# Attention units in nine steps, each at a place between two blocks of the mixture's matmuls

## Chip, cores and metric

One core of one Trainium2 chip runs the whole program. The metric is the device time in microseconds (us), the median of several executions; the profile is of one execution.

## What is computed

Three stages in a row: windowed attention with four sink tokens, a maximum-of-three mixture with an output matrix, and a routed set of eight experts. The change touches the first two.

```python
def _attn_ref(q, k, v, n_sink, window):          # 4 batches, 8 heads, 768 tokens, 64 wide; 4 sinks, window 128
    scores = scale * np.matmul(q, k.transpose(0, 1, 3, 2))
    keep = is_sink | in_window
    scores = np.where(keep, scores, -1000000000.0)
    a = np.exp(scores - np.max(scores, axis=-1, keepdims=True))
    a = a / (np.sum(a, axis=-1, keepdims=True) + 1e-09)
    return np.matmul(a, v)
def _moe_ref(x, w1, w2, w3, w_out):              # x: 3072 tokens x 512
    h = np.maximum(np.maximum(x @ w1, x @ w2), x @ w3)   # 768 wide
    return h @ w_out
def _moe2_ref(x, w_gate, w1, w2):                # 8 experts of 384 tokens each, by descending logit
    ...
        h = np.maximum(x[mask] @ w1[e], 0.0)
        out[mask] = h @ w2[e]
```

## The kernel before

The 3072 tokens are handled as eight groups (0 to 7) of 384 tokens: half a batch each. A group needs four **units** of attention, one for each pair of heads, which give its four tiles `x0` to `x3`, and then its **mixture**. Products are made of fp32r parts: each operand is split into a high part (a rounded copy) and a low part (the rest), and three matmuls stand for one product.

A unit (`att`, L608 to L612) runs through `load` (DMAs of k, q, v and of the sinks' v, `vns`, from the SP queue), `prep` (the splits `kh`, `kz`, `qs` of k and q, `vsp` of v, and on POOL `vk` of the sinks' v, L99 to L102), `score` (six score blocks into PSUM tiles `ps`, copied into `T` by ACT and DVE), `soft` (the row maximum on DVE, six exponentials on ACT, the reciprocal on DVE, the scaling of `T` on POOL) and `pv`. In `pv` TensorE turns `T` into `pt` and `pp`; DVE multiplies `pp` by masks into `A` (L163), ACT copies it into `H`, POOL subtracts into `L`, and TensorE multiplies `H`, `L` and the sinks' part `psb` into `po`, which ACT and DVE write to `x`. `pt`, `pp` and `po` have one PSUM tile each, `ps` three; the tile `A` has one buffer from group 2's units on; `kn`, `qn`, `vn`, `vns` have one buffer each, `H`, `L`, `vsp` and `qs` two.

The mixture of a group is `group` (L249): 18 blocks of 12 matmuls of 384 columns into the two PSUM tiles `mm`, three blocks for each of six slices `f`, the first taken out by ACT (L270) and the others by DVE (L271), after which ACT and DVE split the maximum into `hh` and `hl` (L275, L276). Then comes `x2` (L280): three row tiles times two halves, six blocks of 18 matmuls of 260 columns (L290), each taken out by ACT into `xo` and then by DVE into `LG`; `xo` has one buffer and is stored to `x2d` from SP's queue. Group 0's own `x2` runs after group 1's, from a copy of its maxima that is read back (`reload`, L300: the tile `hm` with two buffers, split by L306 and L307). Groups 6 and 7 make logits first and their `x2` later.

The order within each engine's queue is set by a scheduler that goes through the emitted program by readiness and priority. Before the change the units of group g+1 are emitted whole inside the mixture of group g, ahead of its slices 0, 1, 3 and 4, and with a raised priority of 60 instructions, so that the scheduler may draw their parts forward:

```python
late=list(range(cnt.get(f'a{g+1}',-1)+1,4)) if g+1<NG else []
def between(f):
    if f in spread and late: late.pop(0); emit(f'a{g+1}',True)
```

Of the kernel before, what the change touches and what calls it, by code (L numbers as in the profile page):

```python
# [22 lines left out]
def f32(ap): return ap.bitcast(FT)  # L23
# [3 lines left out]
class Attn:  # L27
# [55 lines left out]
    def prep(s,u):  # L83
# [26 lines left out]
    def score(s,u):  # L110
        nc=s.nc; w=s.w; hf=u['hf']
# [3 lines left out]
        for i in range(3):  # L115
            first = hf==0 and i==0
# [31 lines left out]
    def pv(s,u,x):  # L148
        nc=s.nc; w=s.w; T=u['T'].rearrange('p u j -> p (u j)'); hf=u['hf']; nb=u['nb']; nat=u['nat']
        psk=s.pst.tile([128,512],FT,name="pt")  # L150
        for i in range(3): flip(nc,psk[:,i*128:(i+1)*128],T[:,264*i+128:264*i+256],s.ident)
        PB=s.pb[u['n']%2]
        nc.scalar.activation(PB[0:8],psk[0:8,:384],AF.Copy)
        nc.vector.tensor_tensor(PB[32:40],psk[0:8,:384],f32(PB[0:8]),op=OP.subtract)
# [3 lines left out]
        for h in range(2):  # L158
            pt=s.psp.tile([128,512],FT,name="pp")
            for i in range(3):  # L160
                flip(nc,pt[:,i*128:(i+1)*128],T[:,i*264+136*h:i*264+136*h+128],s.ident)
            A=s.two(dict(n=u['n']*2+h),[128,3,2,128],FT,"A")
            nc.vector.tensor_tensor(A,pt[:,:384].rearrange("p (i q) -> p i q",q=128)[:,:,None,:].to_broadcast([128,3,2,128]),  # L163
                s.ul[:,None,:,:].to_broadcast([128,3,2,128]),op=OP.mult)
            Af=A.rearrange("p i u q -> p (i u q)")
            a=slice(64*h,64*h+64); o=slice(64-64*h,128-64*h)
            if nat:
                if h==0:
                    po=s.psv.tile([128,512],FT,name="po")
                    for a_ in range(2): nc.tensor.matmul(po[:,:384],u['VK'][:,a_,:],PB,start=(a_==0),stop=False,skip_group_check=True)  # L170
                for c,n,q,blk in jobs:
                    nc.tensor.matmul(po[a,q:q+n],u['vn'][:,blk,h,:],Af[:,c:c+n],start=False,stop=True,skip_group_check=True)
                if h==1: nc.scalar.activation(x,po[:,:384],AF.Copy)
                continue
            H=w.tile([128,768],FR,name="H"); L=w.tile([128,768],FR,name="L")
            nc.scalar.activation(H,Af,AF.Copy)  # L176
            nc.gpsimd.tensor_tensor(L,Af,f32(H),op=OP.subtract)  # L177
            po=s.psv.tile([128,512],FT,name="po")
            for part in (H,L):
                for j,(c,n,q,blk) in enumerate(jobs):  # L180
                    nc.tensor.matmul(po[:,q:q+n],u['VS'][:,blk,128*h:128*h+128],part[:,c:c+n],start=(part is H and j==0),stop=False,skip_group_check=True)  # L181
            nc.tensor.matmul(po[:,:384],u['VK'][:,h,:],PB,start=False,stop=True,skip_group_check=True)
            nc.scalar.activation(x[a,:],po[o,:384],AF.Copy)
            nc.vector.tensor_tensor(x[a,:],po[a,:384],x[a,:],op=OP.add)
# [561 lines left out]
```

## Time and profile before

| | |
|---|---|
| median of 3 runs | 1030.28 us (1025.59 to 1030.44) |
| the profiled execution: its own time | 1030.27 us |
| the profiled execution: span of the core | 1028.5 us, mean granted TensorE clock 0.974 |
| busy share of the span: PE, DVE, ACT, POOL | 92%, 69%, 52%, 34% |
| start of group 1's `x2` (first L290 matmul), us from the span's start | 188.44 |
| start of the read-back `x2` of group 0 | 212.34 |
| start of the mixtures of groups 2 to 6 | 244.36, 321.20, 398.03, 468.70, 538.10 |
| start of the `x2` of groups 2 to 5 | 299.05, 373.55, 448.49, 517.69 |
| start of the mixture of group 7 | 582.48 |

The starts are those of the first matmul of each part in the timeline of TensorE. The share of busy time alone doesn't say much here, since the attention and mixture stretches and the later experts have different limits; the table of stretches further down cuts the profile at these starts.

### The profile page before, as it was taken

What the parts mean: (1) busy time and instruction counts of PE and PEld (TensorE: products, weight loads), DVE (VectorE), ACT (ScalarE), POOL (GpSimd) and SP (SyncE); (2) the same over time, 40 slices, a digit from 0 to 9 for tenths busy, and PEclk for the clock granted to TensorE, in tenths of its full rate; (3) what the DMA queues carried; (4) which work ended last, traced back from release to release, by engine and by line L of the source; (5) the groups of instructions that cost most, each with busy time, mean ns of one, the idle gap of its engine ahead of it and who ended that gap; (6) DMA issues with size and microseconds to landing.
All of it is one profiled execution on the core that took longest, in us unless ns stands there. A gap on an engine that the chain in (4) does not pass through costs nothing.

```text
span 1028.5 us, 18554 instructions
## 1 busy us (share of the span) xinstructions
PE 947.7 (92%) x6633; PEld 864.2 (84%) x6633; DVE 711.3 (69%) x1775; ACT 535.8 (52%) x1418; POOL 344.7 (34%) x307
## 2 busy tenths in 40 slices
PE   4879899979999989999999999798989899999996
PEld 3568799879999989989999998786768778788896
DVE  8989876888887884776534344787768788783330
ACT  5667655888788785786452211343333343344431
POOL 4677473145645533435332000101111121133431
PEclk9999999989999999999999999999999999999999
DMA  6543501222112111111010000425243453444420
GB/s 209 156 137 124 164 28 62 74 95 75 46 44 78 48 48 42 54 56 43 13 43 1 1 2 22 149 83 164 84 125 111 134 164 114 132 146 153 154 103 31
DMA packets 47085, 90.32 MB, mean 88 GB/s; under 512 B 6320, under 2 KB 17328, under 8 KB 46992
## 3 DMA queue, kind: packets, MB, share of 16 engines
q1 hardware_dynamic: 42288, 75.11, 23.8%
q0 software_dynamic: 3840, 12.45, 3.5%
q10 hardware_dynamic: 864, 1.57, 0.4%
q8 instruction: 52, 0.85, 0.3%
q14 instruction: 41, 0.34, 0.1%
HBM read 75.48 MB, written 13.76 MB: 87 GB/s over the span
## 4 chain that ended last, share of the span: by engine, by line
PE 61%; DVE 15%; issue 8%; DMA 7%; ACT 6%; POOL 2%; SPq 0%; another core or an unknown queue 0%; POOLq 0%; DVEq 0%; ACTq 0%
PE mm L268 23%; PE mm L576 8%; PE acc L569 8%; PE mm L290 7%; PE po L181 3%; DMA sa<-in_u_dram 2%; PE rc L377 2%; DMA xg<-x2d,idx 2%; PE pt L25 2%; DVE cA L223 1%; DMA st<-in_words_dram 1%; PE pp L25 1%; ACT T_w L144 1%; DVE qs L97 1%; DVE m L141 1%
## 5 line engine op out<-in xcount | busy, mean ns | idle before, releaser
L177 POOL TENSOR_TENSOR L<-A_w,H 128x768 fp32r<-128x768 f32 x46 | 87.5, 1902 | 127.0 <-ACT H L176 98.5
L271 DVE TENSOR_TENSOR hm<-mm,hm 128x384 f32<-128x384 f32 x96 | 53.1, 554 | 61.2 <-PE mm L268 60.1
L290 PE MATMUL mm<-woh,hh 128*128 128x260 f32 (+1 forms) x288 | 85.3, 298 | 5.2 <-DVE LG L293 4.2
L290 PE MATMUL mm<-woh,hl 128*128 128x260 f32 (+1 forms) x288 | 83.7, 295 | 3.9 <-DVE hl L307 2.5
L290 PE MATMUL mm<-wol,hh 128*128 128x260 f32 (+1 forms) x288 | 83.0, 290 | 0.0
L569 PE MATMUL acc<-wbh,hl 128*128 128x512 f32 x192 | 78.0, 406 | 0.5 <-DVE hl L580 0.5
L569 PE MATMUL acc<-wbl,hh 128*128 128x512 f32 x192 | 77.9, 406 | 0.0
L534 POOL DMA_INDIRECT xg<-x2d,idx x24 | 27.4, 1140 | 150.7 <-DVE idx L502 46.6
L569 PE MATMUL acc<-wbh,hh 128*128 128x512 f32 x192 | 77.4, 403 | 0.0
L522 ACT ACTIVATE wah<-sa 128x512 fp32r<-128x512 f32 x64 | 40.4, 631 | 70.1 <-PE mm L576 36.7
L588 POOL DMA_INDIRECT out_dram<-og,idx x24 | 24.5, 1020 | 141.0 <-ACT og L587 138.0
L522 ACT ACTIVATE wbh<-sb 128x512 fp32r<-128x512 f32 x64 | 40.4, 631 | 59.4 <-PE acc L569 54.1
L268 PE MATMUL mm<-xh,w1h 128*128 128x384 f32 x192 | 66.5, 346 | 1.5 <-DVE hm L271 0.7
L580 DVE SCALAR_TENSOR_TENSOR hl<-mm,hh 128x384 fp32r<-128x384 f32 x64 | 35.5, 555 | 46.8 <-ACT hh L579 45.2
L268 PE MATMUL mm<-xh,w2h 128*128 128x384 f32 x192 | 66.5, 347 | 1.4 <-ACT hm L270 1.4
L268 PE MATMUL mm<-xh,w0h 128*128 128x384 f32 x192 | 66.3, 345 | 0.0
L268 PE MATMUL mm<-xl,w0h 128*128 128x384 f32 x192 | 64.9, 338 | 1.2 <-DVE xl L257 1.2
L268 PE MATMUL mm<-xh,w1l 128*128 128x384 f32 x192 | 65.2, 340 | 0.0
L268 PE MATMUL mm<-xl,w1h 128*128 128x384 f32 x192 | 65.2, 339 | 0.0
L268 PE MATMUL mm<-xl,w2h 128*128 128x384 f32 x192 | 64.7, 337 | 0.0
L268 PE MATMUL mm<-xh,w0l 128*128 128x384 f32 x192 | 64.7, 337 | 0.0
L268 PE MATMUL mm<-xh,w2l 128*128 128x384 f32 x192 | 64.6, 337 | 0.0
(308 smaller groups left out, 3103.2 us busy)
## 6 DMA issues: line engine op xcount, KB each, us to landing
sa<-in_u_dram SPq DMA_DIRECT2D x64, 256.0 KB
sb<-in_u_dram SPq DMA_DIRECT2D x64, 256.0 KB
st<-in_words_dram SPq DMA_DIRECT2D x24, 512.0 KB
qn<-in_q_dram SPq DMA_DIRECT2D x24, 192.0 KB
x2d<-xo SPq DMA_DIRECT2D x18, 256.0 KB
kn<-in_k_dram SPq DMA_DIRECT2D x12, 264.0 KB
vn<-in_v_dram SPq DMA_DIRECT2D x12, 256.0 KB
kn<-in_k_dram SPq DMA_DIRECT2D x12, 198.0 KB
```

Source lines behind the costliest of these rows:

```text
L25: nc.tensor.transpose(out,x,f32(ident))
L177: nc.gpsimd.tensor_tensor(L,Af,f32(H),op=OP.subtract)
L181: nc.tensor.matmul(po[:,q:q+n],u['VS'][:,blk,128*h:128*h+128],part[:,c:c+n],start=(part is H and j==0),stop=False,skip_group_check=True)
L268: nc.tensor.matmul(ps[:,:384],s.W[i][a][:,p,f*128:(f+1)*128],X[p][b],start=(n==0),stop=(n==11)); n+=1
L271: else: nc.vector.tensor_tensor(m,ps[:,:384],m,op=OP.max)
L290: nc.tensor.matmul(ps[:,:n],H[f][a][:,t*128:(t+1)*128],s.WO[b][:,f,u,:n],start=(k==0),stop=(k==17)); k+=1
L522: nc.scalar.activation(h,src,AF.Copy)
L534: nc.gpsimd.indirect_dma_start(out=g,out_offset=None,in_=s.x2d[0:first or 3072],in_offset=bass.IndirectOffsetOnAxis(ap=idx[:,t:t+1],axis=0 ...
L569: nc.tensor.matmul(acc[t],H[f][a][:,t*128:(t+1)*128],W[f][1][b],start=(f==0 and n==0),stop=(f==F-1 and n==2)); n+=1
L576: nc.tensor.matmul(ps[:,:384],W[f][0][a][:,k,:],X[k][b],start=(n==0),stop=(n==11)); n+=1
L580: nc.vector.scalar_tensor_tensor(l,ps[:,:384],0.0,f32(h),op0=OP.max,op1=OP.subtract)
L588: st=nc.gpsimd.indirect_dma_start(out=s.out,out_offset=bass.IndirectOffsetOnAxis(ap=idx[:,t:t+1],axis=0),in_=o,in_offset=None)
```

## The change

`pv` is cut into `turned` (the transposes, `A`, `H`, `L`, and now also the making of `vk`) and `pv` proper (the matmuls into `po` and their eviction), each once for each of the pair's two heads, and `score` yields between its three parts. A unit becomes a generator of nine steps: load, prep, three of score (the third with soft), two of turned, two of pv. The steps stand at places 0, 2, 4, 5, 6, 10, 11, 14 and 15 counted from the unit's start; units of groups 3 to 7 start six places apart. A place is the point ahead of one block of the mixture: 18 in `group` and six in `x2`, 24 in a group. What a step emits on TensorE gets an order edge behind the last matmul emitted before it; the raised priority is gone for these units. The read-back `x2` of group 0 has no places. Groups 0 to 2 are emitted as before, apart from the new order of the statements inside a unit.

```diff
     def score(s,u):
...
         for i in range(3):
+            if i: yield
...
+    def turned(s,u,h):
+        nc=s.nc; w=s.w; T=u['T'].rearrange('p u j -> p (u j)'); nat=u['nat']
+        if h==0:
+            VK=u['VK']=s.vk[u['n']%2]
...
+            nc.gpsimd.tensor_copy(hi,u['sv'])
+            nc.gpsimd.tensor_tensor(lo,u['sv'],f32(hi),op=OP.subtract)
+            psk=s.pst.tile([128,512],FT,name="pt")
...
+    def unit(s,b,hf,p,native,main,xs):
+
+        u=s.load(b,hf,p,native); yield
+        s.prep(u); yield
+        yield from s.score(u)
+        s.soft(u); yield
+        s.turned(u,0); yield
+        s.turned(u,1); yield
+        x=main.tile([128,384],FT,name=f"x{p}")
+        s.pv(u,x,0); yield
+        s.pv(u,x,1); xs.append(x)
...
         for f in range(6):
-            if between is not None: between(f)
             m=main.tile([128,384],FT,name="hm",bufs=2)
             for i in range(3):
                 ps=s.mm.tile([128,512],FT,name="mm")
                 n=0
+                if between is not None: between()
...
-    def x2(s,H,t0,LG,x2d,n=260,pool=None,keep=None):
+    def x2(s,H,t0,LG,x2d,n=260,pool=None,keep=None,between=None):
...
+                if between is not None: between()
...
+        todo=[]; clock=[0]
+        STEPS=(0,2,4,5,6,10,11,14,15)
+        def plan(g,start):
+            for p in range(4):
+                U=unit(g,p); todo.extend((start+6*p+t,g,p,U) for t in STEPS)
+            todo.sort(key=lambda x: x[0])
+        def slot(g=None):
+
+            while todo and (todo[0][0]<=clock[0] or any(x[1]==g for x in todo)):
+                with tc.issue_after(M.mm_.ins): next(todo.pop(0)[3],None)
+            if g is None: clock[0]+=1
...
+                    clock[0]=24
+                    for G in range(3,NG): plan(G,24*G-36-6*(G==NG-1))
```

Every engine has as many instructions as before, and up to the start of group 1's `x2` all five queues stand in the same order.

First place, DVE during the read-back of group 0 (`hl3` and `hl4` are low parts of the read-back maxima; `kz`, `qs`, the predicated copies and `m` belong to the splits, scores and row maximum of a unit). Before:

```order
L307 TENSOR_TENSOR hl3_2313<-hm_2310,hh3_2312 128x384
L135 COPY_PREDICATED T_w_2672<-ca_95,ps_2688 128x128
L95 TENSOR_TENSOR kz0b_1618<-kn_3030,kh0_x_3038 64x528
L135 COPY_PREDICATED T_w_2672<-ca_95,ps_2693 128x128
L97 TENSOR_TENSOR qs0_3040<-qn_3032,qs0_3040 64x384
L95 TENSOR_TENSOR kz1b_1619<-kn_3030,kh1_x_3039 64x528
L163 TENSOR_TENSOR A_w_1846<-pp_1842,ul_98 128x768
L135 COPY_PREDICATED T_w_2672<-ca_95,ps_2698 128x128
L97 TENSOR_TENSOR qs1_3041<-qn_3032,qs1_3041 64x384
L154 TENSOR_TENSOR psb0_105<-pt_2548,psb0_105 8x384
L141 TENSOR_REDUCE m_2703<-T_w_2672 128x6
L307 TENSOR_TENSOR hl4_2319<-hm_2316,hh4_2318 128x384
```

And with the change, same engine and place:

```order
L327 TENSOR_TENSOR hl3_2456<-hm_2453,hh3_2455 128x384
L158 TENSOR_TENSOR psb0_105<-pt_2346,psb0_105 8x384
L164 TENSOR_TENSOR A_w_1835<-pp_1831,ul_98 128x768
L327 TENSOR_TENSOR hl4_2462<-hm_2459,hh4_2461 128x384
L327 TENSOR_TENSOR hl5_2468<-hm_2465,hh5_2467 128x384
```

Eight DVE instructions of group 3's units have left the stretch between `hl3` and `hl4`; TensorE has 24 score matmuls fewer between the read-back `x2`'s start and the mixture of group 2.

Second place, TensorE in the `x2` of group 3, from the end of its first two blocks (`hl5` closes both) to the third block (`mm_4201`, which takes the PSUM tile of the first). Before:

```order
L290 MATMUL mm_4178<-woh_1466,hl5_4153 128x260
L181 MATMUL po_4414<-H_4410,vsp_4328 128x128
L181 MATMUL po_4414<-H_4410,vsp_4328 128x256 x2
L181 MATMUL po_4414<-H_4410,vsp_4328 128x128
L181 MATMUL po_4414<-L_4411,vsp_4328 128x128
L181 MATMUL po_4414<-L_4411,vsp_4328 128x256 x2
L181 MATMUL po_4414<-L_4411,vsp_4328 128x128
L182 MATMUL po_4414<-psb0_105,vk0_103 128x384
L126 MATMUL ps_5423<-kh1_x_5398,qs1_5400 128x132
L127 MATMUL ps_5423<-kz1b_1619,qs1_5400 128x132
L126 MATMUL ps_5428<-kh0_x_5397,qs0_5399 128x260
L127 MATMUL ps_5428<-kz0b_1618,qs0_5399 128x260
```

And with the change:

```order
L310 MATMUL mm_4234<-woh_1466,hl5_4178 128x260
L189 MATMUL po_4259<-H_4115,vsp_3841 128x256 x2
L189 MATMUL po_4259<-H_4115,vsp_3841 128x128
L310 MATMUL mm_4257<-woh_1466,hh0_3643 128x260
L310 MATMUL mm_4257<-wol_1467,hh0_3643 128x260
L310 MATMUL mm_4257<-woh_1466,hl0_3644 128x260
```

The score matmuls ahead of the third block are gone, and the matmuls into `po` are cut in two, the second part inside the fourth block.

Third place, TensorE in the mixture of group 4 with the change, between two blocks and inside the next (`ps` are scores of one unit, `po` belongs to an older one):

```order
L287 MATMUL mm_4582<-xh3_4474,w1l_121 128x384
L124 MATMUL ps_4636<-kh0_w_4521,qs0_4523 128x260
L125 MATMUL ps_4636<-kz0_111,qs0_4523 128x260
L287 MATMUL mm_4625<-xh0_4462,w2h_122 128x384
L287 MATMUL mm_4625<-xl0_4463,w2h_122 128x384
L287 MATMUL mm_4625<-xh0_4462,w2l_123 128x384
L124 MATMUL ps_4641<-kh1_w_4522,qs1_4524 128x260
L125 MATMUL ps_4641<-kz1_112,qs1_4524 128x260
```

Pieces of a unit that stood next to each other before, several score blocks at once, now come one or two at a time between or inside blocks.

## Rows read from the trace of the kernel before

**Rows 1.** Stretches from group 1's `x2` to group 7's mixture, cut at the starts above

```profile
core 0: us, PE busy (x) PEld busy (x) DVE busy (x) ACT busy (x) POOL busy (x), PEclk, DMA share, GB/s
188.44:212.34 23.90, 21.20 (x158) 20.20 (x157) 19.53 (x38) 20.45 (x66) 9.69 (x7) 0.93 0.24 70
212.34:244.36 32.02, 26.23 (x179) 24.14 (x178) 26.53 (x48) 25.82 (x76) 13.24 (x11) 0.89 0.30 93
244.36:299.05 54.69, 54.69 (x364) 54.37 (x363) 46.34 (x93) 42.79 (x118) 30.67 (x28) 1.00 0.16 47
299.05:321.20 22.15, 20.84 (x169) 20.17 (x168) 18.00 (x40) 20.81 (x67) 10.03 (x8) 1.00 0.27 85
321.20:373.55 52.35, 51.88 (x328) 50.72 (x327) 43.47 (x76) 38.36 (x114) 24.37 (x20) 1.00 0.17 47
373.55:398.03 24.48, 21.96 (x157) 20.99 (x156) 14.05 (x36) 17.44 (x54) 9.56 (x9) 0.86 0.20 60
398.03:448.49 50.46, 50.46 (x328) 50.29 (x326) 36.23 (x72) 35.12 (x101) 19.78 (x19) 1.00 0.16 46
448.49:468.70 20.21, 18.51 (x147) 17.52 (x146) 13.65 (x32) 15.95 (x46) 8.83 (x7) 1.00 0.20 61
468.70:517.69 48.99, 48.99 (x314) 48.71 (x313) 30.26 (x55) 30.86 (x94) 20.07 (x17) 1.00 0.08 24
517.69:538.10 20.41, 18.73 (x142) 18.41 (x142) 7.68 (x17) 8.02 (x18) 8.59 (x8) 0.92 0.13 41
538.10:582.48 44.38, 44.38 (x271) 43.52 (x270) 19.60 (x60) 13.72 (x26) 6.65 (x7) 1.00 0.02 7
```

**Rows 2.** What TensorE waited for from 188.44 to 582.48: us in total, times, longest us

```profile
PE mm L290 <- DVE LG L293: 4.2, 5, 1.2
...
PE ps L126 <- DVE T_w L135: 2.4, 4, 1.2
```

**Rows 3.** Timeline, `x2` of group 3: start us, us, engine, instruction [idle before <-releaser]

```profile
382.26 0.58 PE L126 MATMUL ps<-kh_x,qs 128*128 128x260 f32 x1 [1.22 <-DVE T_w L135]
...
382.82 0.98 DVE L141 TENSOR_REDUCE m<-T_w 128x6 f32<-128x792 f32 x1
...
383.92 0.58 PE L290 MATMUL mm<-woh,hh 128*128 128x260 f32 x1 [0.86 <-DVE LG L293]
```

**Rows 4.** Timeline of the read-back

```profile
216.68 0.55 DVE L307 TENSOR_TENSOR hl<-hm,hh 128x384 fp32r<-128x384 f32 x1
216.72 0.86 SPq L304 DMA_DIRECT2D hm<-sp  x2
...
224.20 2.67 DVE L307 TENSOR_TENSOR hl<-hm,hh 128x384 fp32r<-128x384 f32 x2
...
226.92 0.80 PE L290 MATMUL mm<-woh,hl 128*128 128x260 f32 x2 [0.45 <-DVE hl L307]
```

**Rows 5.** Timeline of DVE and POOL, second half of the read-back stretch

```profile
232.69 1.50 POOL L147 TENSOR_TENSOR T_w<-T_w,l 128x792 f32<-128x792 f32 x1
...
232.79 3.65 DVE L95 TENSOR_TENSOR kz<-kn,kh_w 64x396 fp32r<-64x396 f32 x1 [0.87 <-ACT kh_w L94]
...
234.16 1.85 POOL L177 TENSOR_TENSOR L<-A_w,H 128x768 fp32r<-128x768 f32 x1
```

**Rows 6.** Chain of waits, read-back: start us, us, what

```profile
213.50 2.31 DMA hm<-sp
...
221.74 0.95 ACT hh L306 x2
```

**Rows 7.** Chain of waits, `x2` of group 2

```profile
315.14 4.30 PE mm L290 x36
319.44 0.64 PE po L181 x6
...
320.31 0.33 PE pp L25 x3
320.64 0.12 PE ps L126
```

More of the change, by code (lines that the diff above doesn't have):

```diff
@@ L157, in pv @@
         for i in range(3): jobs.append((i*256+128,256 if i<2 else 128,i*128,i+hf))
[L158 to L184, printed above, removed]
@@ new lines, in pv @@
+        a=slice(64*h,64*h+64); o=slice(64-64*h,128-64*h)
+        if nat:
+            if h==0:
+                u['po']=s.psv.tile([128,512],FT,name="po")
+                for a_ in range(2): nc.tensor.matmul(u['po'][:,:384],u['VK'][:,a_,:],PB,start=(a_==0),stop=False,skip_group_check=True)
+            for c,n,q,blk in jobs:
+                nc.tensor.matmul(u['po'][a,q:q+n],u['vn'][:,blk,h,:],u['A'][h][0][:,c:c+n],start=False,stop=True,skip_group_check=True)
+            if h==1: nc.scalar.activation(x,u['po'][:,:384],AF.Copy)
+            return
@@ new lines, in pv @@
+        po=s.psv.tile([128,512],FT,name="po")
+        for n_,part in enumerate(u['A'][h]):
+            for j,(c,n,q,blk) in enumerate(jobs):
+                nc.tensor.matmul(po[:,q:q+n],u['VS'][:,blk,128*h:128*h+128],part[:,c:c+n],start=(n_+j==0),stop=False,skip_group_check=True)
+        nc.tensor.matmul(po[:,:384],u['VK'][:,h,:],PB,start=False,stop=True,skip_group_check=True)
+        nc.scalar.activation(x[a,:],po[o,:384],AF.Copy)
+        nc.vector.tensor_tensor(x[a,:],po[a,:384],x[a,:],op=OP.add)
@@ L590, in expert, with attention_mixtures @@
             s.scat.append(st)
[L592 removed]
+def attention_mixtures(tc,q,k,v,vs,words,wg,u1,u2,out,off=60,native=8,order='a0 a0 a0 a0 w a1 a1 w w w w w a1 a1 a2',order1='a2 o o o o o o a2 a2',back=1,at=(1,0),s1=300,s2=400,nring=6):
     nc=tc.nc
@@ L607, in attention_mixtures, with unit @@
         NG=8; xs={}; cnt={}
+        def unit(g,p): return A.unit(g//2,g%2,p,4*g+p<native,main,xs.setdefault(g,[]))
         def att(g,p):
-            xs.setdefault(g,[])
-            u=A.load(g//2,g%2,p,4*g+p<native); A.prep(u); A.score(u); A.soft(u)
-            x=main.tile([128,384],FT,name=f"x{p}")
-            A.pv(u,x); xs[g].append(x)
+            for _ in unit(g,p): pass
+        todo=[]; clock=[0]
[8 more added lines that the diff above has]
+            if g is None: clock[0]+=1
         def lw(f): M.load_w(f)
@@ L635, in attention_mixtures @@
                     for o in order1.split(): emit(o,True)
-                late=list(range(cnt.get(f'a{g+1}',-1)+1,4)) if g+1<NG else []
-                def between(f):
-                    if f in spread and late: late.pop(0); emit(f'a{g+1}',True)
+                    clock[0]=24
+                    for G in range(3,NG): plan(G,24*G-36-6*(G==NG-1))
                 if g<2:
-                    while late: between(spread[0])
+                    for p in range(cnt.get(f'a{g+1}',-1)+1,4): emit(f'a{g+1}',True)
+                slot(g)
                 d = g>=NG-2
@@ L647, in attention_mixtures @@
                     r=Route(tc,LG,rt,rw,rc)
-                H6,H=H if g==NG-1 else None,M.group(xs[g],sp if g==0 else None,hp if g==NG-1 else None,rest,between)
-                while late: between(spread[0])
+                H6,H=H if g==NG-1 else None,M.group(xs[g],sp if g==0 else None,hp if g==NG-1 else None,rest,slot if g else None)
                 rest=None
@@ L653, in attention_mixtures @@
                     if g==NG-1: r.bids((0,21),True)
-                elif g: M.x2(H,3*g,LG,x2d)
+                elif g: M.x2(H,3*g,LG,x2d,between=slot)
                 if g==back:
```

36 lines of the change are left out of this document (22 added, 14 removed).

## The prediction

> **What bounds the kernel now.** I read the page's busy shares first, then cut the time in which the changed order runs, from group 1's `x2` at 188.44 us to group 7's mixture at 582.48 us, into its parts [rows 1]. Ahead of it and behind it the program is the same. In each line, length minus PE's busy time is TensorE's idle time. Two kinds of stretch show. The five mixture stretches (54.69, 52.35, 50.46, 48.99, 44.38 us) hold TensorE busy all the time but for 0.47 us in one of them: there it is the bound, and nothing but fewer matmuls would help. The six `x2` stretches are idle for 2.70, 5.79, 1.31, 2.52, 1.70 and 1.68 us, 15.7 us together. In four of them the granted clock is below 1.00 as well: 0.93, 0.89, 0.86 and 0.92. The clock has two levels, 2.4 and 1.2 GHz, so a mean of 0.89 over 32.02 us costs 0.11 × 32.02 = 3.5 us; the four give 1.7, 3.5, 3.4 and 1.6, together 10.2 us. What can be won at all is thus 16.2 + 10.2 = 26.4 us of 394.
>
> What ends the idle time is DVE in nearly every case: the `LG` copy that frees a PSUM tile of `x2`, 4.2 us, and the predicated copies that free a score tile [rows 2]. The timeline of group 3's `x2` shows why DVE is late: a score matmul stands in TensorE's queue ahead of the third block and waits 1.22 us for a predicated copy; then a row maximum of 0.98 us stands ahead of `LG` on DVE, and the block waits 0.86 us more [rows 3]. In the read-back the second pair of `hl` comes 7 us after the first [rows 4].
>
> **The change, part by part.** The sum is made against the profiled execution's own 1030.27 us, which lies on the median of the three runs (1030.28).
>
> *Instruction counts.* Nothing is added or removed on any engine, and the order edges are between instructions of TensorE alone, so they carry no semaphore. Cost 0 in themselves.
>
> *Group 1's `x2` (2.70 us idle, 1.7 us of clock).* The attention pieces there are nearly the same in number (20 score matmuls for 18) and order. I take 0; both ends ±1 us, about what its parts idle.
>
> *The read-back stretch (32.02 us).* Ahead of `hl4` eight DVE instructions go. What remains late is the DMA: the loads of the last two `hm` are issued by 217.58 us [rows 4], one takes 2.31 us and one `hh` 0.48 (0.95 for two) [rows 6], so `hl4` can start at 220.4 instead of 224.20: 3.8 us earlier. Then, from 226.92 to 244.36, TensorE took 17.4 us; with the change there remain two rows of 36 matmuls at 4.30 us, seven into `po` at 0.64/6, six transposes at 0.33/3 and four of scores at 0.12 [rows 7], 10.5 us, and one `LG` wait of 1.0: 11.5, so 5.9 less. But the work that left is not gone: 24 score matmuls (2.9 us), six transposes (0.7) and nine into `po` (1.0), 4.6 us, run later where TensorE is the bound and pay in full. Gain 3.8 + 5.9 − 4.6 = 5.1 us. This still has TensorE idle while it waits for the `hm` loads, with fewer pieces to fill the time, so I charge half of the clock loss that this stretch shows, 1.7. Taken: 3.4; ends 1.6 (the whole 3.5) and 5.1.
>
> *The `x2` of groups 2 to 5 (7.2 us idle, 5.0 us of clock).* Two or three attention pieces remain between the first pair of blocks and the third, and they are matmuls into `po` whose operands were made some places earlier; the scores that waited are gone from there. What stays is the structure: both first blocks close on `hl5`, and the third needs ACT's `xo` and DVE's `LG`. I take 1.0 us of idle in each (the longest `LG` wait is 1.2 [rows 2], with about 0.5 us of `po` to cover it, and something for `hl5`) and no lowered clock, since the stretches with 1.31 and 1.70 us idle kept 1.00 [rows 1]; the one with 1.68 did not. Taken 12.2 − 4.0 = 8.2; ends 3.0 and 12.2.
>
> *The mixture stretches.* Here the change can only keep what is there. Before, units also stood inside these stretches and TensorE lost 0.47 us in 251. A step's operands have three or four blocks of over 2 us between being made and being used. DVE, busy 85% in the fullest stretch (46.34 of 54.69), gets a more even load, since the units no longer crowd into the earlier ones; groups 5 and 6 get more, where DVE is busy 7.68 of 20.41 and 19.60 of 44.38 [rows 1]. Taken 0; the ends are in the rivals.
>
> *`vk` moved to `turned`.* The next load of `vns` waits on SP until then, about four places longer, and stores of `xo` stand behind it in SP's queue. In the new order it is the third store of an `x2` that can be held; its buffer is next written a group later. 0.
>
> *The end.* The last `po` of group 7 now stands two blocks ahead of group 7's mixture; the two blocks and ten logit matmuls, over 5 us, hide two evictions and two splits of about 0.55 us each. 0.
>
> Sum: 3.4 + 8.2 = 11.6 us, 1030.27 − 11.6 = **1018.7 us**.
>
> **A rule weighed against rows.** Behind the row maximum and the `LG` copy stands a third cause of late DVE work: in the read-back a `kz` took 3.65 us, starting just after POOL's scaling of `T` (1.50 us) and ending about 0.5 us after the `L` that POOL began next (1.85 us); a DVE instruction here waited through both POOL instructions [rows 5]. Its two POOL neighbours and some 0.3 us of its own make up the 3.65.
>
> The Trainium skill states this as a rule (SBUF — State Buffer, "SBUF: two separate sides"): DVE with two SBUF inputs and GpSimd share a pair of ports that one of them holds for a whole instruction. The row agrees.
>
> By the rows alone, POOL's instructions, `L` twice and `T` once for each unit, are as many after the change as before; so in the sum they change nothing, but with pieces at fixed places a late DVE result has less other work to hide behind. That is the rival on the other side.
>
> **The rivals.** (1) *Places that come too early: slower.* TensorE takes its queue in order, so a step whose operand is late stops all later blocks, in stretches that lose nothing now. What would make it late is a DVE instruction held beside POOL, as in rows 5, ahead of the copy that a score or `po` matmul needs. Price: the longest such wait for a score tile is 1.2 us [rows 2]; once for each of 20 units it is 24 us, which with the gains above gives 1018.7 + 24 = 1042.7. It cancels the gain from 11.6/20 = 0.58 us for each unit. Against it: the even load, and no such loss in 251 us of mixture. Chance 0.10.
>
> (2) *No change.* The idle time of `x2` is its own chain (`hl5`, `xo`, `LG`), not the units'; what was filler is gone, and it is paid for later. Then the four `x2` stretches give only the 3.0, and the read-back 1.6 less a second wait for `LG` of 1.0: 3.6 us, 1026.7. For it: `LG` is the largest wait, and fewer pieces stand there to fill it. Against it: the timeline, where scores and the row maximum make `LG` late. Chance 0.18.
>
> (3) *More.* All idle time and clock loss behind 212.34 us goes but the clock's 1.7 and one us of idle in the read-back: 26.4 − 4.4 (group 1's `x2`) − 2.7 = 19.3 us, 1011.0. For it: four idle spots cause the clock's falls, and both would go together. Against it: the eviction chain. Chance 0.20.
>
> The Trainium skill says of the clock that a busy TensorE releases its throttle and an idle one returns to it (TensorE: Matmul & The Clock Gate, "What's actually happening"). The four lowered stretches, all with idle time, agree; the two idle ones at 1.00 show that not every gap is followed by a fall.
>
> **How the numbers follow.** The forecast itself has 0.52 and reaches from 1013 to 1025: bounds of the read-back and `x2` (4.6 to 17.3 us) drawn in a little at the low end. A measurement can tell about 0.5%, 5.15 us, from no change, so faster means below 1025.1. Faster: 0.52 + 0.20 = 0.72; same: 0.18; slower: 0.10. The range for 8 in 10 goes from the ceiling, 1030.27 − 26.4 = 1003.9, to 1030; beyond it lies the slow rival and little else.
>
> **What would show it.** In the changed profile, cut in the same way: mixture stretches idle below 0.5 us each; `x2` of groups 2 to 5 idle about 1 us each at clock 1.00, with no score wait ahead of the third block; the read-back stretch near 24 us, `hl4` at about 220 us; the later mixtures longer by the deferred pieces. Wrong if score, `po` or `pp` matmuls wait on DVE, ACT or POOL inside mixture stretches, if `LG` waits grow, or if the clock falls in stretches that were at 1.00.

## The result, and the profile after

The changed kernel takes 1045.76 us (median of 4 runs, 1039.98 to 1046.04), the kernel before, run beside it, 1027.93 (4 runs). The ratio is 1.0145, 95% interval 1.0112 to 1.0178: slower by 1.5%, where 1018.7 us and faster were forecast. A second session gave 1.0092 (e9 below). The profiled run took 1045.6 us, 15.3 more than that of before. On the page, TensorE is busy for nearly as long as before (947.7 us then), and DVE too (711.3 then):

```profile
span 1043.7 us, 18517 instructions
...
PE 952.3 (91%) x6633; PEld 869.3 (83%) x6633; DVE 710.8 (68%) x1775; ACT 539.7 (52%) x1418; POOL 343.7 (33%) x307
```

The instruction counts are as before, and the busy times differ by 5 us at most: no engine got more work, TensorE stands idle for longer. The table of stretches, cut at the same places as in [rows 1], shows where:

```profile
190.03:215.91 25.88, 21.43 (x159) 20.40 (x158) 19.14 (x40) 21.31 (x68) 10.67 (x8) 0.93 0.25 73
215.91:235.96 20.05, 17.60 (x140) 16.64 (x139) 11.70 (x21) 10.26 (x21) 9.81 (x8) 1.00 0.29 98
235.96:290.92 54.96, 52.84 (x330) 52.38 (x329) 37.16 (x71) 37.50 (x108) 19.03 (x18) 0.97 0.13 41
290.92:311.52 20.60, 18.31 (x152) 17.90 (x151) 13.97 (x31) 13.87 (x40) 8.76 (x8) 1.00 0.17 56
311.52:363.78 52.26, 50.60 (x323) 49.94 (x322) 38.77 (x76) 36.74 (x105) 19.25 (x18) 1.00 0.15 43
363.78:382.95 19.17, 17.32 (x143) 16.96 (x142) 11.89 (x27) 14.47 (x42) 8.27 (x8) 1.00 0.23 73
382.95:436.31 53.36, 52.38 (x337) 51.66 (x336) 39.96 (x73) 38.19 (x109) 22.34 (x20) 1.00 0.14 41
436.31:458.60 22.29, 19.72 (x151) 19.31 (x150) 14.87 (x33) 13.71 (x40) 9.95 (x10) 0.92 0.19 63
458.60:514.32 55.72, 51.65 (x322) 50.09 (x321) 42.10 (x79) 40.01 (x112) 16.46 (x15) 1.00 0.15 45
514.32:541.95 27.63, 23.09 (x174) 22.47 (x174) 18.59 (x38) 19.74 (x62) 13.93 (x9) 0.88 0.10 37
541.95:595.80 53.85, 51.45 (x325) 49.97 (x323) 28.89 (x79) 26.65 (x73) 20.21 (x19) 1.00 0.05 17
```

Lengths alone mislead, since the change moves attention matmuls from the early stretches into the late ones. What moves cancels if one counts a **loss** for each stretch: its idle time (length minus PE's busy time) plus what the clock took (length times 1 minus the mean granted clock). For the read-back of before that is 5.79 + 0.11 × 32.02 = 9.3. With the five mixtures, and the four `x2` of groups 2 to 5, each taken together (us):

| kernel | group 1's `x2` | read-back | mixtures | `x2` of groups 2 to 5 | sum |
|---|---|---|---|---|---|
| before | 4.4 | 9.3 | 0.5 | 12.2 | 26.4 |
| after | 6.3 | 2.4 | 12.9 | 16.4 | 38.0 |

The difference of the sums, 11.6, is that of the stretches' lengths (405.77 − 394.04 = 11.7), so TensorE's own work has stayed the same. The rest of the 15.2 us between the spans lies ahead of these stretches (1.6) and behind them (1.9). That rest says little: in the profiles of all runs told of below the part behind the stretches takes between 434.8 and 450.6 us. The read-back gained more than forecast; the mixtures, which lost 0.5 us, lose 12.9; and the `x2` got worse, not better.

What TensorE waited for from 190.03 to 595.80 us (total, times, longest):

```profile
PE mm L287 <- DVE hm L290: 6.6, 4, 2.2
PE pp L25 <- POOL T_w L145: 4.5, 1, 4.5
PE mm L310 <- DVE hl L295: 4.3, 3, 1.8
PE mm L310 <- DVE LG L313: 3.4, 2, 2.7
PE mm L287 <- ACT hm L289: 2.1, 2, 1.4
...
PE mm L310 <- ACT hh L294: 1.6, 2, 1.1
```

Against [rows 2], the waits for `LG` and for the predicated copies of a score tile have shrunk (`ps` for `T_w`, 2.4 then, has 0.8 in the same view). In their place stand waits that were absent or small (0.4 us for `hm`, 1.3 for `hl`): for the mixture's own running maximum `hm`, for the mixture's last low part `hl`, and one long wait for POOL's scaling.

**Wait one: `hm`, once in each of four mixtures.** The timeline of group 5's mixture, POOL, DVE and TensorE:

```profile
481.94 1.98 POOL L170 TENSOR_TENSOR L<-A_w,H 128x768 fp32r<-128x768 f32 x1 [3.76 <-ACT H L169]
...
482.22 2.12 DVE L295 TENSOR_TENSOR hl<-hm,hh 128x384 fp32r<-128x384 f32 x1
...
484.26 0.96 DVE L139 TENSOR_REDUCE m<-T_x 128x6 f32<-128x792 f32 x1
485.15 0.54 DVE L290 TENSOR_TENSOR hm<-mm,hm 128x384 f32<-128x384 f32 x1
...
485.74 0.45 PE L287 MATMUL mm<-xh,w0h 128*128 128x384 f32 x1 [2.20 <-DVE hm L290]
```

An `hl` of 128x384 takes 0.55 us in [rows 4]; here it takes 2.12, for it came 0.28 us after POOL's `L` had begun and ended 0.42 after `L` had. Behind it on DVE stand a unit's row maximum and then the `hm` that empties a PSUM tile of the mixture. The next block needs that tile and cannot start for 2.20 us. In group 2's mixture it is the same pattern with nothing else in between:

```profile
276.94 2.19 POOL L170 TENSOR_TENSOR L<-A_w,H 128x768 fp32r<-128x768 f32 x1 [2.90 <-ACT H L169]
277.49 2.06 DVE L295 TENSOR_TENSOR hl<-hm,hh 128x384 fp32r<-128x384 f32 x1
279.47 0.55 DVE L290 TENSOR_TENSOR hm<-mm,hm 128x384 f32<-128x384 f32 x1
...
280.07 0.64 PE L287 MATMUL mm<-xh,w0h 128*128 128x384 f32 x1 [2.12 <-DVE hm L290]
```

In group 3's mixture the wait is 1.36 us, right behind a `qs` of 2.23 us; in group 4's it is 0.87, and the held instruction, a `kz` of 1.85 us, stands six instructions further ahead in a DVE queue without a gap.

Such holds are not new. Counted one by one in the trace of these stretches, DVE subtractions of two operands in SBUF that take over 1.2 us each number 22 before (41.7 us together) and 22 after (40.5 us); 12 of the 22 before lay in mixtures. There one of them looked like this:

```profile
256.00 1.85 POOL L177 TENSOR_TENSOR L<-A_w,H 128x768 fp32r<-128x768 f32 x1 [3.17 <-ACT H L176]
256.03 2.24 DVE L276 TENSOR_TENSOR hl<-hm,hh 128x384 fp32r<-128x384 f32 x1
...
258.92 0.54 DVE L271 TENSOR_TENSOR hm<-mm,hm 128x384 f32<-128x384 f32 x1
...
262.83 0.34 PE L268 MATMUL mm<-xh,w0h 128*128 128x384 f32 x1
```

The block that needs the tile comes 3.4 us after `hm` is done, since pieces of a unit stand on TensorE between the blocks. New is that blocks of the mixture wait behind a held instruction.

**Wait two: POOL's scaling, in the `x2` of group 5.** Two units lie on top of each other here. Group 6's units start at 24 × 6 − 36 = 108, then 114, 120 and 126; group 7's, which start six places earlier than the rule for the others, at 24 × 7 − 42 = 126. So the last unit of group 6 and the first of group 7 start at the same place and take all nine steps together. The scalings of their `T` stand one behind the other on POOL:

```profile
515.66 1.52 POOL L145 TENSOR_TENSOR T_w<-T_w,l 128x792 f32<-128x792 f32 x1
...
522.27 0.19 DVE L144 RECIPROCAL l<-l 128x6 f32<-128x6 f32 x1
...
522.54 2.03 POOL L145 TENSOR_TENSOR T_w<-T_w,l 128x792 f32<-128x792 f32 x1 [5.37 <-DVE l L144]
...
524.62 0.90 PE L25 MATMUL pp<-ident,T_w 128*128 128x128 f32 x3 [4.45 <-POOL T_w L145]
```

POOL itself is free for 5.37 us before the second scaling: it waits for DVE's reciprocal (the second row), which comes 7.9 us after that of the first unit (514.33); the second unit's exponentials on ACT start 9.7 us after the first's. But its transposes stand in TensorE's queue as if the two came together: 4.45 us of idle time, and a mean clock of 0.88 in that stretch.

**Wait three: the mixture's last `hl`.** In the first blocks of group 2's `x2`, where before two matmuls into `po`, three transposes and six scores stood and now two scores and three transposes do:

```profile
295.89 0.96 DVE L164 TENSOR_TENSOR A_w<-pp,ul 128x768 f32<-128x768 f32 x1
...
297.09 0.55 DVE L97 TENSOR_TENSOR qs<-qn,qs 64x384 fp32r<-64x384 f32 x1
297.68 0.56 DVE L295 TENSOR_TENSOR hl<-hm,hh 128x384 fp32r<-128x384 f32 x1
...
298.29 0.51 PE L310 MATMUL mm<-woh,hl 128*128 128x260 f32 x2 [1.80 <-DVE hl L295]
```

### The profile page after: what moved, and what is told of

Its sections match the earlier page's. It is cut to its first block, busy times and chain, and to the rows that moved or that the text cites. A ratio compares the mean times of both kernels' runs of the same rounds, so it can differ in the third digit from the quotient of the medians.

```text
span 1043.7 us, 18517 instructions
## 1 busy us (share of the span) xinstructions
PE 952.3 (91%) x6633; PEld 869.3 (83%) x6633; DVE 710.8 (68%) x1775; ACT 539.7 (52%) x1418; POOL 343.7 (33%) x307
## 4 chain that ended last, share of the span: by engine, by line
PE 61%; DVE 14%; issue 8%; ACT 8%; DMA 7%; POOL 1%; SPq 0%; POOLq 0%; DVEq 0%; ACTq 0%
PE mm L287 22%; PE mm L596 9%; PE acc L589 8%; PE mm L310 7%; PE po L189 3%; PE rc L397 2%; DMA xg<-x2d,idx 2%; PE pt L25 2%; DMA st<-in_words_dram 2%; PE pp L25 1%; DVE qs L97 1%; DVE cA L242 1%; PE ps L124 1%; DMA sb<-in_u_dram 1%; PE ps L125 1%
## 5 line engine op out<-in xcount | busy, mean ns | idle before, releaser
L542 ACT ACTIVATE wbh<-sb 128x512 fp32r<-128x512 f32 x64 | 40.4, 631 | 62.2 <-PE acc L589 58.6
L600 DVE SCALAR_TENSOR_TENSOR hl<-mm,hh 128x384 fp32r<-128x384 f32 x64 | 35.5, 555 | 47.1 <-ACT hh L599 42.8
```

The costliest lines, as they stand in the source:

```text
L542: nc.scalar.activation(h,src,AF.Copy)
L600: nc.vector.scalar_tensor_tensor(l,ps[:,:384],0.0,f32(h),op0=OP.max,op1=OP.subtract)
```

## The experiments

The theory after the result has two causes: the two units at place 126 (crowding), and units six places apart, a quarter of a group's 24, so that in every group the same instruction of the mixture meets POOL's `L` (the exposed hold). Rivals: steps too close behind their operands altogether, the order edges, the lost priority. Any edit lets the scheduler order all queues anew, so a run is an edit and its new order together; that is a limit on all that follows. Medians of the kernel before differ by sessions (1022.1 to 1028.0 us), so ratios are compared.

**e1: five apart at the seam.** Units of group 6 start at 107, 112, 117, 122, those of group 7 at 127, 132, 137, 142.

```diff
-        def plan(g,start):
+        def plan(g,start,gap=6):
...
-                U=unit(g,p); todo.extend((start+6*p+t,g,p,U) for t in STEPS)
+                U=unit(g,p); todo.extend((start+gap*p+t,g,p,U) for t in STEPS)
...
-                    for G in range(3,NG): plan(G,24*G-36-6*(G==NG-1))
+                    for G in range(3,NG): plan(G,24*G-36-(G==6)-5*(G==NG-1),6-(G>5))
```

> Only the starts of the units of groups 6 and 7 change: 107, 112, 117, 122 and 127, 132, 137, 142 in place of 108 to 126 and 126 to 144, so that no two units start at one place. Theory A (two units at place 126 crowd ACT, DVE and POOL in group 5's mixture and x2): the stretches from group 5's mixture to group 6's mixture lose most of the 12.8 us that they have over before beyond the moved work; time 1033 to 1037 us beside 1046. Theory B (places as such are too rigid: each group's mixture waits for a DVE eviction held beside POOL): the crowded stretches stay as idle as they are, 1043 to 1047.

**e2: no shift for group 7.** All 20 units six apart, none at the same place.

```diff
-                    for G in range(3,NG): plan(G,24*G-36-6*(G==NG-1))
+                    for G in range(3,NG): plan(G,24*G-36)
```

> Group 7's units start six places later, at 132 to 150, as the rule for the other groups has it; the last steps of its last unit are then forced out just ahead of group 7's mixture. Theory A: group 5's mixture and x2 get back about 9 us, and group 7's mixture waits some 3 to 5 us at its start for its last tile: 1037 to 1041. Theory B: no gain, and the wait at group 7's start on top: 1047 to 1050.

Measured: e1 1029.06 us, ratio 1.0059 (1.0032 to 1.0085); e2 1030.38, ratio 1.0056 (1.002 to 1.0092). Both take part of the loss away, neither all. Of e2, the largest wait, and the rows of group 5's mixture and `x2` and of group 6's mixture:

```profile
PE mm L287 <- DVE hm L290: 6.6, 4, 2.2
```

```profile
456.52:511.80 55.28, 52.74 (x322) 51.55 (x321) 38.84 (x75) 37.10 (x105) 18.13 (x16) 0.97 0.14 40
511.80:530.99 19.19, 17.35 (x144) 16.99 (x143) 11.90 (x27) 14.48 (x42) 8.26 (x8) 1.00 0.23 74
530.99:583.68 52.69, 52.69 (x342) 51.69 (x341) 34.07 (x62) 33.30 (x96) 20.71 (x16) 1.00 0.05 15
```

The wait for POOL's scaling is gone; the `x2` of group 5 has 1.84 us of idle time in place of 4.54 and a clock of 1.00, and group 6's mixture none in place of 2.40. The waits for `hm` stand as they were, four of them, 6.6 us. So the two causes are separate, and this run takes one. In e1 the wait for POOL's scaling is gone as well, but the `x2` of group 5 still idles 3.90 us at a clock of 0.87, 3.44 of it at a transpose that waits for DVE's `A`: taking the double start away was not enough there.

**e3: the units of groups 3 to 6 six places earlier.** Group 7's stay, so that all starts are six apart and none meet.

```diff
-                    for G in range(3,NG): plan(G,24*G-36-6*(G==NG-1))
+                    for G in range(3,NG): plan(G,24*G-42)
```

> All units of groups 3 to 7 start six places earlier, group 7's as in the changed kernel, so that units start six apart throughout. Theory A: the double start is gone, 1033 to 1038, unless units crowd in group 1's mixture instead, where group 2's units still run. Theory B: 1043 to 1047.

Measured: 1045.11 us, ratio 1.0209 (1.0179 to 1.0239), worse than the change itself, and slower by its ratio than either theory had it: a miss. In the profile the read-back is long again, 30.33 us with 5.80 idle at a clock of 0.89, for 173 of PE's instructions stand in it in place of 140; each `x2` of groups 2 to 5 idles for 2.5 to 4.3 us, that of group 5 for 4.27 without a double start. So the double start is not the only thing that can make that stretch idle, and starting earlier doesn't help.

**e4: no order edges.**

```diff
-                with tc.issue_after(M.mm_.ins): next(todo.pop(0)[3],None)
+                next(todo.pop(0)[3],None)
```

> The same nine steps at the same places, without the order edge on TensorE: the scheduler may draw their matmuls ahead. Theory A: the crowding stays, so little changes: 1040 to 1047. Theory B: the edge is what makes TensorE wait at fixed places; without it the waits in the mixture stretches (11 us idle there) fall to a few us: 1033 to 1039.

Measured: 1033.84 us, ratio 1.0102 (1.0073 to 1.013), no better than the change in e9 (1.0092). But two things moved against each other under that total. The read-back takes 32.50 us again, 6.00 of it idle, as before the change (32.02, 5.79): what shortened it is the edges, which hold the steps of group 3's units out of it, and not the cutting into steps. And the five mixtures idle for 2.2 us together in place of 11.2, as the second theory had it, though 21 DVE instructions are held (42.8 us). Of the wait for `hm` this is left:

```profile
PE mm L287 <- DVE hm L290: 1.0, 2, 0.8
```

So the same edges that win the read-back are part of what lets the held instructions be felt in the mixtures. What that would give, the read-back and the `x2` of groups 2 to 5 take: the loss of these `x2` is 23.1 us for 16.4, with clocks of 0.82 and 0.83 in two of them.

**e5 and e6: no hold by `L`.** POOL's `L` is written by two memsets, which read nothing, so the low part's share of the output is left out; e5 on the changed kernel, e6 on the kernel before.

```diff
-            nc.gpsimd.tensor_tensor(L,Af,f32(H),op=OP.subtract)
+            nc.gpsimd.memset(f32(L),0.0); nc.gpsimd.memset(f32(L),0.0)
```

> The changed kernel with POOL's low part L written by two memsets instead of the subtraction: POOL is about as long at it but reads no operand, so the products are of H alone and the output is not the reference's. Theory B1 (a DVE instruction with two SBUF operands waits out an L of 1.9 us, and the mixture's eviction behind it comes late): the recurring wait for hm goes, the mixture stretches' 11 us of idle time fall to about 3, and the time to 1034 to 1039 on a chip where the changed kernel has 1.0145 of before (that is, 1.005 to 1.010 of before). Theory A alone (double start only): no change, 1.013 to 1.016.

> The same memsets for L in the kernel before: control. Theory B1: before has no idle time in its mixture stretches to win, only part of the 15.7 us in its x2 stretches: 0.992 to 0.998 of before, less than what the changed kernel gains by the same edit. If the edit gains as much here as there, the lock is not what sets the two apart.

Measured: e5 1023.33 us, ratio 0.9997 (0.9979 to 1.0015); e6 1015.14, ratio 0.9921 (0.9892 to 0.9949). In group 2's mixture of e5, at the place of the fence above, an `hl` beside POOL is no longer stretched:

```profile
270.34 0.56 DVE L295 TENSOR_TENSOR hl<-hm,hh 128x384 fp32r<-128x384 f32 x1
270.45 1.54 POOL L170 MEMSET L<- 128x768 f32 x2 [2.67 <-PE po L189]
```

The mixtures idle for 1.4 us together in place of 11.2, while the wait of the crowded place stays (`pp` for `T_w`, 4.7 us). So without the hold nearly all idle time in the mixtures goes, 9.8 us. The causes overlap: e2, where the holds stand, took 4.0 of the same 11.2, and e4 took 9.1. The edit is worth 0.8% to the kernel before and 0.9 to 1.5% to the changed one (whose ratio is 1.0092 or 1.0145 by session): the difference, 0.2 to 0.7%, is what the change added in exposure. The edit also shortens POOL's work (1.54 us in place of 1.9) and frees it of its wait for `H`, so this is an upper bound. Only the holds by `L` go: in e6 11 held instructions are left, 18.5 us, beside POOL's scaling of `T` and its `vsp`.

**e7: the hold cut in three.** The changed kernel, nothing left out.

```diff
-        nc.gpsimd.tensor_tensor(L,Af,f32(H),op=OP.subtract)
+        [nc.gpsimd.tensor_tensor(L[:,c:c+256],Af[:,c:c+256],f32(H[:,c:c+256]),op=OP.subtract) for c in (0,256,512)]
```

> The changed kernel with L made by three subtractions of 256 columns instead of one of 768, nothing left out. Theory B1: a DVE instruction waits out 0.7 us instead of 1.9, so the waits for hm shrink to a third: 1.008 to 1.012 of before. Theory A alone: 1.013 to 1.017, as three instructions cost POOL a little more.

Measured: 1028.38 us, ratio 1.0077 (1.0045 to 1.0108). Held DVE instructions of over 1.2 us fall from 22 to 5 (10.8 us), the wait for `hm` from 6.6 to 1.9. Against 1.0145 that is 0.7%; against e9's 1.0092 it is within the intervals.

**e8: even starts.** The 20 units start evenly from place 36 to 144, 5.7 apart; no two meet, and none keeps a fixed position in the group.

```diff
-                U=unit(g,p); todo.extend((start+6*p+t,g,p,U) for t in STEPS)
+                U=unit(g,p); todo.extend((36+round((4*g-12+p)*108/19)+t,g,p,U) for t in STEPS)
...
-                    for G in range(3,NG): plan(G,24*G-36-6*(G==NG-1))
+                    for G in range(3,NG): plan(G)
```

> All 20 units start at even distances from place 36 to place 144, 5.7 places apart, in place of six apart with one double start. Theory A: no crowding anywhere and no forced end, so like the two earlier versions without the double start or a little better: 1.002 to 1.007 of before. Theory B1 (fixed places meet POOL's L): waits of about 2 us a group remain, at other blocks.

Measured: 1024.28 us, ratio 1.001 (0.9991 to 1.0029): the loss is gone. The rows of the five mixtures, and the largest waits:

```profile
232.59:284.50 51.91, 51.76 (x336) 51.21 (x334) 36.46 (x70) 37.50 (x109) 18.73 (x18) 1.00 0.14 44
...
308.61:360.13 51.52, 50.41 (x321) 49.92 (x322) 37.00 (x74) 37.65 (x110) 21.11 (x19) 1.00 0.16 47
...
386.28:437.23 50.95, 50.95 (x330) 50.77 (x329) 36.84 (x68) 35.73 (x103) 20.45 (x20) 1.00 0.14 44
...
459.88:509.80 49.92, 49.92 (x319) 49.66 (x319) 38.65 (x75) 38.04 (x107) 21.00 (x18) 1.00 0.17 50
...
531.26:581.57 50.31, 50.31 (x322) 49.31 (x321) 30.16 (x79) 25.60 (x71) 18.85 (x15) 1.00 0.04 12
```

```profile
PE mm L310 <- DVE LG L313: 5.1, 4, 2.9
PE mm L310 <- DVE hl L295: 3.5, 2, 2.4
```

The mixtures idle for 1.3 us, with POOL's `L` as it was and 25 DVE instructions still held (43.2 us): the holds are there, but hardly a block of a mixture waits for them. The `x2` of groups 2 to 5 now lose 13.2 us of idle time and 3.5 of clock: against the kernel before (4.2 and 1.3), the waits for `LG` and `hl` have grown.

**e9 to e12: one session.** The changed kernel as it is; with the raised priority for its steps; the kernel before with `L` in thirds; even starts with `L` in thirds (the edits of e8 and e7 together).

```diff
-                with tc.issue_after(M.mm_.ins): next(todo.pop(0)[3],None)
+                with tc.issue_after(M.mm_.ins),tc.high_priority(offset=off): next(todo.pop(0)[3],None)
```

> The changed kernel as it is, in the session of the next three, so that they can be compared with it and not only with the kernel before. The median of the kernel before has been 1022 to 1028 us in the sessions so far. If the loss belongs to the program, the ratio is 1.0112 to 1.0178 again and the same waits stand in the profile: T_w of POOL ahead of pp for over 4 us, hm in four of the mixture stretches. If the session moves the ratio by more than 0.5%, the finer comparisons of single edits with each other across sessions fall.

> The changed kernel, but each step is emitted with the raised priority of 60 instructions that the units had before; places and order edges stay. Theory (places and crowding decide, not priority): the step's work on DVE, ACT and POOL is drawn forward a little, but two units still start at place 126 and the instructions beside POOL's L still hold hm, so 1040 to 1046 us by the kernel before at 1028, ratio 1.011 to 1.018. Rival (the lost priority is what makes T_w and hm late): with it back the waits of pp on T_w and of the mixture on hm go, some 11 us, ratio 1.000 to 1.005. A ratio above 1.018 would say that steps drawn forward stand ahead of the mixture's evictions and make them later.

> The kernel before, but POOL's L is made in three subtractions of 256 columns, nothing left out. A DVE instruction with two SBUF operands that comes while POOL subtracts is then held for a third of 1.9 us. Leaving L out altogether took 0.8% from the kernel before (ratio 0.9921). Theory (the hold ends with POOL's instruction): some of that is won, 0.993 to 0.998, with the idle time in the x2 stretches below 1.5 us each. Rival (POOL's total time counts, or the shorter pieces wait more often): 0.998 to 1.004.

> The changed kernel with its 20 units of groups 3 to 7 started evenly from place 36 to 144 (5.7 places apart, no two at one place), and POOL's L in three subtractions of 256 columns. Even starts alone gave 1.001 [0.9991, 1.0029]; the thirds alone took 1.0145 to 1.0077. Theory (two separate causes, crowding and the exposed hold): what is left of the hold at even starts, hm waits of 2.3 and hl of 3.5 us, falls by half, ratio 0.994 to 0.999. Rival (the even starts had already hidden the hold): 0.999 to 1.003. Above 1.003 the thirds would cost something of their own.

| run | us | ratio to the kernel before |
|---|---|---|
| e9, the change | 1039.68 | 1.0092 (1.0059 to 1.0125) |
| e10, with priority | 1039.08 | 1.0099 (1.007 to 1.0128) |
| e11, before, thirds | 1025.85 | 0.9972 (0.9946 to 0.9998) |
| e12, even starts, thirds | 1026.16 | 0.9954 (0.9928 to 0.9981) |

e9's ratio fell 0.5% short of the first session's: the change is slower by 0.9 to 1.5%, and single steps of under 0.5% across sessions are not told apart. Its profile shows the same waits (`hm` 6.6 us in 4, `T_w` 4.4 in 1). e10 rules the priority out. In its profile the wait of the crowded place comes on another instruction, `po` for `H`, with 4.6 us in place of 4.4. e11 and e12 gain a little, as the theory had it, and lie within each other's intervals; e12's median is the lowest against the kernel before of all runs that leave nothing out. The `x2` in e11 idle for 1.6 to 2.6 us each, though, where under 1.5 was expected. `L` in thirds costs POOL a little: from the first piece's start to the last one's end 2.1 to 2.9 us, where one piece took 1.9.

**e13 and e14: what stands in the way of a gain.** Even starts with the memsets of e5; even starts without the edges (the edit of e4).

> The changed kernel with even starts of its units (place 36 to 144) and POOL's L written by two memsets, which read nothing, in place of the subtraction; so the products of L are zeros and those of H stay. The same edit of L gave 0.9921 [0.9892, 0.9949] on the kernel before and 0.9997 [0.9979, 1.0015] on the changed kernel with its own starts. Theory (two separate causes, two units at place 126 and the exposed hold; with both gone the places give the gain in the read-back and little else): no idle time over 0.3 us in any mixture stretch, ratio 0.985 to 0.990, below the kernel before with the same edit. Rival (even starts and the removed hold cure the same waits; nothing is left to gain): 0.991 to 0.997, with the x2 stretches idle for 3 us or more as with even starts alone, where LG and the mixture's last hl are waited for.

> The changed kernel with even starts of its units, but without the order edges; the steps are emitted at the same places. On the changed kernel's own starts the edges' removal gave 1.0102 [1.0073, 1.013] against 1.0092 to 1.0145 with them, and brought the long read-back stretch back (32.50 us). Theory (the edges only pay where the read-back is; the crowded starts made the rest): the read-back is 30 us or more again with 4 to 6 us idle, and the ratio is 1.003 to 1.009, worse than even starts with edges (1.001). Rival (the edges hold TensorE back at a late operand): without them the scheduler orders around it, 0.993 to 1.000.

Measured: e13 1014.69 us, ratio 0.9911 (0.9888 to 0.9935), which is no different from e6, the kernel before with the same edit (0.9921). The median is on the rival's side of the border, and the mixtures' idle time, up to 0.88 us in one, is more than the theory's 0.3; the rival's sign, `x2` idle for 3 us or more, shows in one of four. e14 1031.51, ratio 1.0086 (1.0059 to 1.0113), as the theory had it; its read-back:

```profile
212.78:245.41 32.63, 25.84 (x181) 24.02 (x180) 27.43 (x49) 25.64 (x76) 13.20 (x11) 0.90 0.30 91
```

Losses of all these, counted as above (us; e10, which is like the change, is left out):

| kernel | group 1's `x2` and read-back | mixtures | `x2` of groups 2 to 5 | sum |
|---|---|---|---|---|
| before | 13.7 | 0.5 | 12.2 | 26.4 |
| after | 8.7 | 12.9 | 16.4 | 38.0 |
| e9, the change again | 6.6 | 11.2 | 16.6 | 34.4 |
| e1, five apart | 6.3 | 7.5 | 19.4 | 33.2 |
| e2, no shift | 6.0 | 8.9 | 13.8 | 28.7 |
| e3, earlier | 13.6 | 8.3 | 24.0 | 45.9 |
| e4, no edges | 15.2 | 2.2 | 23.1 | 40.4 |
| e8, even starts | 6.3 | 1.3 | 16.7 | 24.3 |
| e14, even, no edges | 14.4 | 2.3 | 19.5 | 36.2 |
| e11, before, thirds | 12.2 | 0.0 | 14.9 | 27.1 |
| e7, after, thirds | 9.3 | 7.0 | 18.2 | 34.6 |
| e12, even, thirds | 8.9 | 2.5 | 10.3 | 21.7 |
| e6, before, no hold | 12.9 | 0.0 | 6.0 | 18.9 |
| e5, after, no hold | 5.6 | 1.4 | 20.0 | 27.0 |
| e13, even, no hold | 7.5 | 1.1 | 8.2 | 16.8 |

These are single profiles, and two of the same program (after and e9) differ by 3.5 us in the sum; but the stretches' lengths follow the ratios. Against before they are longer by 19.4 us in e3, 11.4 in e4 and 8.8 in e7 and shorter by 8.4 in e6 and 11.1 in e13, where the ratios stand for 21.4, 10.4, 7.9, −8.1 and −9.1; furthest off is e2, 1.9 for 5.7. Down the first column, the nine steps with edges save 5 to 8 us (3 with thirds), but for e3. Down the third, the versions of the nine steps lose more than the kernel before with the same `L`: 13.8 to 24.0 for 12.2, and without the hold 8.2 and 20.0 for 6.0; of the thirds, e7 loses 18.2 and e12 10.3 for 14.9. In idle time alone, without the clock, there is no exception (e12 8.6 for 7.9). That is where most of the gain goes.

## Why the prediction was wrong

- *Instruction counts, 0.* Right for the counts: PE, DVE, ACT and POOL are busy for what they were, and the stretches' lengths differ by their losses alone. But that the order edges cost 0 in themselves leaves out the order they force: without them the mixtures idle for 2.2 us in place of 11.2 (e4).
- *Group 1's `x2`, 0 ± 1.* The loss rose by 1.9 in the profile shown (4.45 us idle) and by 0.3 in e9's. Within what one profile can tell.
- *The read-back, 3.4 (1.6 to 5.1).* Right in its mechanism and too small: its loss fell by 6.9. The last pair of `hl` starts at 223.28 in the timeline below, 7.37 us after the stretch's start; 220.4 was forecast for a start at 212.34, so 8.1. The clock did not fall, where the prediction charged 1.7 us for it, and idle time fell by 3.3 us. Two waits make up 2.08 of the 2.45 us that are left, and the longer one is once more behind a held `hl`, the first row:

```profile
218.05 2.20 DVE L327 TENSOR_TENSOR hl<-hm,hh 128x384 fp32r<-128x384 f32 x1
...
220.31 0.39 PE L310 MATMUL mm<-woh,hl 128*128 128x260 f32 x1 [1.79 <-DVE hl L327]
...
223.28 1.03 DVE L327 TENSOR_TENSOR hl<-hm,hh 128x384 fp32r<-128x384 f32 x2 [0.92 <-ACT hh L326]
...
223.30 0.39 PE L310 MATMUL mm<-woh,hh 128*128 128x260 f32 x1 [0.29 <-ACT hh L326]
```

- *The `x2` of groups 2 to 5, 8.2 (3.0 to 12.2).* Wrong, 12.3 us from what was measured. "I take 1.0 us of idle in each ... and no lowered clock": measured 2.29, 1.85, 2.57 and 4.54 us, and clocks of 0.92 and 0.88 in the last two, a loss of 16.4 for 12.2. The 4.54 is the crowded place. In the others the waits of the scores shrank as forecast, and that for `LG` a little, but the waits for the last `hh` and `hl`, 1.3 us before, became 5.9: the chain that rival (2) named, `hl`, `xo`, `LG`. Rival (2)'s reason, that the pieces which left were filler, is not shown: in the `x2` of groups 2 to 4 of e8 146 matmuls of units stand where the kernel before has 149, and yet they idle for 11.7 us in place of 5.5. Without the hold by `L` they idle for 5.0 (e13, 3.1 in e6), so part of it is the hold again; the cause of the rest stays open.
- *The mixtures, "Taken 0".* The other step that failed, 12.4 us; with the 3.5 us that the read-back gained beyond its forecast and the 1.9 of group 1's `x2`, these two lead, to within 0.2 us, from the forecast gain of 11.6 us to the 11.7 lost. Two things were overlooked. "A step's operands have three or four blocks ... between being made and being used" looked at the units' operands; the operand that came late is the mixture's own `hm`, which waits in DVE's queue behind a held instruction. And DVE's "more even load" did not lay the 20 starts side by side: 24G − 36 and the six of group 7 give 126 twice.
- *A rule weighed against rows; rival (1).* The hold was named, with the right rows [rows 5] and a time, 1042.7, that lies 3 us from the first session's median and from e9's. That nearness is luck. Its chance, 0.10, was too low, and its price was put together otherwise: not 1.2 us for each of 20 units on a score tile, but 0.9 to 2.2 us once in each of four mixtures on `hm`, and the crowded place on top. "No such loss in 251 us of mixture" was no evidence against it: 12 held DVE instructions lay in the mixtures before, and no block of a mixture was held up by them. The Trainium skill's rule (SBUF — State Buffer, "SBUF: two separate sides") says that the pair of ports is held for a whole instruction, and by DVE with two SBUF inputs only against a GpSimd instruction that reads SBUF. The runs agree: beside a memset `hl` takes 0.56 us in place of 2.06 (e5), and with pieces of a third 5 held instructions are left of 22 (e7).
- *`vk` and the end, 0.* No wait for either shows among TensorE's. Ahead of and behind the stretches 3.5 us were added, less than profiles differ there (the part ahead takes 187.1 to 190.2 us in the runs that leave `L` as it is).

What is settled, as far as runs with a new order each can settle it: the holds by `L` are needed for the idle time in the mixtures (e5), and so are the fixed starts (e8) and the edges (e4); take any one away and 9 to 10 of the 11.2 us go. The double start makes the wait for POOL's scaling in group 5's `x2` (gone in e1, e2 and e3), and the edges are what shortens the read-back (e4, e14). What stays open is the size of each in time, since the causes overlap: crowding 0.4 to 0.9% (e2), even starts another 0.5% in another session (e8 against e2), with intervals of 0.3%. Open, too, is why the `x2` of groups 2 to 5 idle for longer in every version of the nine steps than in the kernel before with the same `L`.

## What to carry to other kernels

When steps are put at fixed places in an in-order queue, lay all their starts side by side first, the seams between loops above all. Ask whether their distance divides the period of what they run beside: a fixed ratio can repeat the same collision in every round, as six of 24 did here together with order edges (5.7 did not, in e8). Ask for each instruction that comes late not only who uses its result, but what stands ahead of it in its own engine's queue and whether that is held. And count a gain in one stretch together with what the same edit does to the others: the edges that shortened the read-back were part of what cost the mixtures as much and more.

## What was not expected of the hardware

A DVE instruction with both operands in SBUF that meets POOL's `L` lasts until after its end, up to 2.23 us in place of 0.55 (`qs`, `hl`). In the whole trace of the changed kernel 25 of them start while an `L` runs, and all 25 end 0.41 to 0.57 us after it; of DVE's two-operand arithmetic that reads a PSUM tile 19 instructions start beside an `L`, and none takes over 0.56 us. A hold is not yet a cost: the kernel before has 22 in the stretches, 41.7 us of DVE time in 394, and taking those beside `L` away (11 are left) gave at most 0.8% (e6, which shortens POOL's work too). Cut in three, POOL's `L` takes 0.2 to 1.0 us longer in all and leaves 5 to 13 long holds in place of 22 to 25, for 0.3% of the time in the kernel before (e11) and 0.6% with even starts (e12 against e8, in different sessions, which differ by nearly as much).
